# Sliding-window attention and a SwiGLU block: softmax denominators pre-added and inverted as exp(-ln), SiLU as one function, projection and scores in one phase, weights cast by DMA

## Chip, cores, metric

One core of one Trainium2 chip. The metric is the device time of the program in microseconds (us); lower is better. The span in a profile is a little shorter than that time (496.8 against 498.5 us in the profiled run of the changed kernel).

## The reference

```python
# q, k, v: (8, 8, 576, 64) float32;  x: (4608, 512);  w_gate, w_val: (512, 1536);  w_out: (1536, 512)
scores = matmul(q, k^T) / 8
scores = where((0 <= i - j) & (i - j < 64), scores, -1e9)      # causal window of 64
attn = exp(scores - max);  attn = attn / (sum(attn) + 1e-9)
x = matmul(attn, v), heads side by side, batches below one another   # 4608 tokens x 512
g = x @ w_gate
out = (g / (1 + exp(-g)) * (x @ w_val)) @ w_out
```

## The kernel before

The 4608 tokens are nine tiles of 512. A tile has four head pairs. For a head pair, GpSimd casts q, k and v to bf16, TensorE transposes q and k, VectorE puts the keys block-diagonally into `kbd`, TensorE makes the scores, ScalarE takes exp, GpSimd multiplies by a mask, and TensorE makes the product with v and, with a matrix of ones, the denominators:

```python
    def products(u):
        ...
        d_ps = ps_a.tile([P, 512], FP32, name="ad_ps", tag="a")
        for c in range(2):
            nc.tensor.matmul(d_ps[:], bones[:], E[:, :, c, :], start=(c == 0), stop=(c == 1))
        r = att.tile([P, 512], FP32, name="r", tag="r")
        nc.vector.reciprocal(r[:], d_ps[:])
        nc.vector.tensor_mul(xT[t][:, p, :], o_ps[:], r[:])

    def gate_value(t, m):            # 12 per tile; 8 matmuls of 512 columns each
        ...
        nc.scalar.activation(th[:], g_ps[:], AF.Tanh, scale=0.5)
        nc.vector.scalar_tensor_tensor(sg[:], th[:], 1.0, g_ps[:], ALU.add, ALU.mult)
        nc.vector.tensor_mul(hT[t][:, m, :], sg[:], v_ps[:])     # 0.5 is in w_out

    def project(t, s, pool, tag):    # 4 per tile; 12 matmuls of 512 columns
        ...
        nc.scalar.copy(os_[:], o_ps[:])
        nc.sync.dma_start(out[...], os_[:])
```

The main loop has 36 slots, four per tile. Each slot mixes everything, so that each engine has a little of each kind of work (the slots of the first tile, which also load and cast the weights, are cut):

```python
    for w in range(NU):              # NU = 36
        t, s = divmod(w, 4)
        ...
        gate_value(t, 3 * s)
        if w + 4 < NU: products(w + 4)
        gate_value(t, 3 * s + 1)
        if w + 5 < NU: transposes(w + 5)
        project(t - 1, s, ps_o, "o")
        if w + 8 < NU: load(w + 8)   # three to four slots ahead of its use
        if w + 6 < NU: casts(w + 6)
        if w + 5 < NU: scores(w + 5)
        gate_value(t, 3 * s + 2)
```

The softmax here doesn't subtract the row's maximum and nothing guards it: scores larger than these inputs give would overflow.

## Time and profile before

| | before |
|---|---|
| time, median of 3 runs | 472.12 us (470.81 to 472.59) |
| span of the profile | 468.9 us |
| TensorE (PE), VectorE (DVE), ScalarE (ACT), GpSimd (POOL) busy | 78, 72, 31, 38% |
| one slot, one tile, in steady state | 11.54 us, 46.2 us |

From the page, the busy time of each engine, and its time in 40 slices:

```profile
PE 367.7 (78%) x2332; PEld 189.3 (40%) x2332; DVE 338.8 (72%) x380; ACT 145.2 (31%) x253; POOL 176.9 (38%) x258
...
PE   1453866738888888888888888888888888889996
...
DVE  7188798777777777777777777777777777776540
```

Matmuls are pipelined, so a busy PE is not a PE at its peak: a matmul of 512 columns is shown with some 0.38 us, but such matmuls start 0.216 us apart (four in 0.86 us).

From the timeline of one steady slot (columns: start, duration, engine, line, operation, output<-input, count, and in brackets the idle time before it and who ended it):

```profile
256.67 3.35 DVE L217 RECIPROCAL r<-ad_ps 128x512 f32<-128x512 f32 x1
...
258.36 2.75 PE L242 MATMUL o_ps<-wo,hT 128*128 128x512 bf16 x12
...
260.06 0.69 DVE L218 TENSOR_TENSOR xT<-ao_ps,r 128x512 bf16<-128x512 f32 x1
260.67 0.68 DVE L236 SCALAR_TENSOR_TENSOR sg<-th,g_ps 128x512 f32<-128x512 f32 x1
...
262.05 0.41 DVE L152 COPY kbd_94<-tp 64x512 bf16<-64x512 bf16 x1
262.47 0.43 DVE L153 COPY kbd_94<-tp 64x512 bf16<-64x512 bf16 x1
...
262.96 0.37 PE L175 MATMUL s_ps<-qT,kbd_94 128*128 128x128 bf16 x4 [1.81 <-DVE kbd_94 L153]
```

The reader sees one reciprocal take 3.35 us, VectorE do everything after it late, and TensorE stand 1.81 us waiting for the two key copies at the end of that queue. The groups and the waits say the same over the whole run (a group: busy us, mean ns of one, then idle before it and its releaser; a wait: us in total, times, longest):

```profile
L217 DVE RECIPROCAL r<-ad_ps 128x512 f32<-128x512 f32 x36 | 120.7, 3353 | 5.0 <-PE ad_ps L215 5.0
```
```profile
PE s_ps L175 <- DVE kbd_93 L153: 31.6, 16, 4.8
PE s_ps L175 <- DVE kbd_94 L153: 29.2, 15, 2.7
```

### The profile page before, as it was taken

How to read it: one execution, taken by the hardware profiler on the slowest of the kernel's cores; microseconds unless marked ns; L12 is line 12 of the kernel's file. 1: busy time of each engine (PE TensorE's matmuls, PEld its weight loads, DVE VectorE, ACT ScalarE, POOL GpSimd, SP SyncE). 2: the span in 40 equal slices, each digit the busy share in tenths (PEclk: the TensorE clock that was granted, in tenths of full speed). 3: DMA queues.
4: the chain of work that ended last, by engine and by line, in shares of the span. 5: the costliest groups of instructions: out<-in, count | busy, mean ns of one | idle time of the engine just before them, and what ended most of it. 6: DMA issues, size and time to landing. Idle time of an engine off the chain costs nothing.

```text
span 468.9 us, 6826 instructions
## 1 busy us (share of the span) xinstructions
PE 367.7 (78%) x2332; PEld 189.3 (40%) x2332; DVE 338.8 (72%) x380; ACT 145.2 (31%) x253; POOL 176.9 (38%) x258
## 2 busy tenths in 40 slices
PE   1453866738888888888888888888888888889996
PEld 0331433414444444444444444444444444444443
DVE  7188798777777777777777777777777777776540
ACT  1220222313333333333333333333333333323232
POOL 3873445424444444444444444444444433110000
PEclk9975897879999999999999999999999999999999
DMA  7965567741332355333333443233343330001012
GB/s 173 253 182 130 154 183 209 219 104 46 87 87 67 79 138 124 87 76 82 87 86 92 119 111 90 70 90 92 90 113 92 91 89 24 22 24 45 22 46 89
DMA packets 129314, 47.65 MB, mean 102 GB/s; under 512 B 119040, under 2 KB 123136, under 8 KB 129280
## 3 DMA queue, kind: packets, MB, share of 16 engines
q1 hardware_dynamic: 129280, 47.22, 39.3%
q8 instruction: 18, 0.29, 0.3%
q14 instruction: 16, 0.13, 0.1%
HBM read 37.75 MB, written 9.44 MB: 101 GB/s over the span
## 4 chain that ended last, share of the span: by engine, by line
DVE 52%; PE 35%; ACT 4%; SPq 3%; issue 2%; POOL 2%; DMA 1%; DVEq 0%; POOLq 0%; ACTq 0%
DVE r L217 24%; PE g_ps L229 14%; PE v_ps L229 9%; DVE hT L237 9%; DVE sg L236 8%; PE o_ps L242 6%; DVE xT L218 5%; PE s_ps L175 4%; ACT th L234 3%; SPq L88 2%; POOL E L183 2%; DVE kbd_93 L153 1%; DVE kbd_94 L153 1%; DVE kbd_93 L152 1%; PE ad_ps L215 1%
## 5 line engine op out<-in xcount | busy, mean ns | idle before, releaser
L183 POOL TENSOR_TENSOR E<-E,mask 128x512 bf16<-128x512 bf16 (+1 forms) x72 | 84.5, 1185 | 215.4 <-ACT E L180 215.4
L236 DVE SCALAR_TENSOR_TENSOR sg<-th,g_ps 128x512 f32<-128x512 f32 x108 | 73.9, 684 | 86.5 <-ACT th L234 86.4
L217 DVE RECIPROCAL r<-ad_ps 128x512 f32<-128x512 f32 x36 | 120.7, 3353 | 5.0 <-PE ad_ps L215 5.0
L229 PE MATMUL g_ps<-xT,wg 128*128 128x512 bf16 x432 | 115.4, 391 | 2.9 <-DVE xT L218 2.9
L229 PE MATMUL v_ps<-xT,wv 128*128 128x512 bf16 x432 | 114.3, 388 | 0.0
L234 ACT ACTIVATE th<-g_ps 128x512 f32<-128x512 f32 x108 | 64.5, 597 | 128.4 <-PE g_ps L229 128.4
L242 PE MATMUL o_ps<-wo,hT 128*128 128x512 bf16 x432 | 98.6, 379 | 0.0
L237 DVE TENSOR_TENSOR hT<-sg,v_ps 128x512 bf16<-128x512 f32 x108 | 74.2, 687 | 11.6 <-PE v_ps L229 0.6
L229 PEld LDWEIGHTS <-wv 128*128 128x128 bf16 x432 | 43.3, 100 | 57.2 <-issue 8.6
L180 ACT ACTIVATE E<-s_ps 128x512 bf16<-128x512 f32 (+1 forms) x72 | 39.1, 592 | 68.6 <-PE s_ps L175 68.6
L242 PEld LDWEIGHTS <-hT 128*128 128x128 bf16 x432 | 41.1, 98 | 44.6
L229 PEld LDWEIGHTS <-wg 128*128 128x128 bf16 x432 | 40.9, 100 | 44.5 <-issue 3.5
L175 PE MATMUL s_ps<-qT,kbd_93 128*128 128x128 bf16 (+1 forms) x160 | 14.0, 232 | 33.0 <-DVE kbd_93 L153 31.6
L149 ACT COPY qT<-tp 128x512 bf16<-128x512 bf16 x36 | 21.1, 586 | 45.6 <-PE tp L147 45.6
L175 PE MATMUL s_ps<-qT,kbd_94 128*128 128x128 bf16 (+1 forms) x128 | 10.3, 224 | 29.2 <-DVE kbd_94 L153 29.2
L147 PE MATMUL tp<-identb,q_b 128*128 128x128 bf16 x144 | 14.8, 229 | 16.9 <-POOL q_b L108 16.9
L215 PE MATMUL ad_ps<-E,bones 128*128 128x512 bf16 x72 | 23.1, 405 | 5.4 <-DVE r L217 5.4
L175 PEld LDWEIGHTS <-kbd_93 128*128 128x128 bf16 x160 | 10.8, 107 | 39.1 <-DVE kbd_93 L153 36.3
L218 DVE TENSOR_TENSOR xT<-ao_ps,r 128x512 bf16<-128x512 f32 x36 | 24.9, 692 | 1.2
L108 POOL CAST q_b<-q_f 128x512 bf16<-128x512 f32 x36 | 22.7, 630 | 6.1 <-DMA q_f<-in_q_dram 4.5
L109 POOL CAST k_b<-k_f 128x512 bf16<-128x512 f32 x36 | 22.1, 613 | 4.3 <-PE g_ps L229 3.3
L147 PEld LDWEIGHTS <-q_b 128*128 128x128 bf16 x144 | 11.3, 102 | 26.0 <-POOL q_b L108 18.2
(77 smaller groups left out, 240.7 us busy)
## 6 DMA issues: line engine op xcount, KB each, us to landing
w_f<-in_moe_w_gate_dram SPq DMA_DIRECT2D x4, 768.0 KB, 5.4
w_f<-in_moe_w_val_dram SPq DMA_DIRECT2D x4, 768.0 KB, 7.1
q_f<-in_q_dram SPq DMA_DIRECT2D x32, 96.0 KB, 3.8
k_f<-in_k_dram SPq DMA_DIRECT2D x32, 96.0 KB, 2.4
wo_f<-in_moe_w_out_dram SPq DMA_DIRECT2D x4, 768.0 KB, 6.0
q_f<-in_q_dram SPq DMA_DIRECT2D x16, 128.0 KB, 2.8
k_f<-in_k_dram SPq DMA_DIRECT2D x16, 128.0 KB, 3.2
v_f<-in_v_dram SPq DMA_DIRECT2D x16, 128.0 KB, 3.2
```

The lines of the kernel that those rows point to most:

```text
L147: nc.tensor.transpose(tp[:, i, P * c:P * c + P], x[:, c, :], identb[:])
L175: nc.tensor.matmul(s_ps[:, 64 + P * i:64 + P * i + n], kbd[t % 2][:, p, j, :], qT[:, 64 * j:64 * j + n],)
L180: nc.scalar.activation(Ef[:, 512 * h + lo:512 * h + 512], s_ps[:, lo:512], AF.Exp, scale=0.125)
L183: nc.gpsimd.tensor_mul(Ef[:, 512 * h + lo:512 * h + 512], Ef[:, 512 * h + lo:512 * h + 512], mask[:].rearrange("r m c x -> r (m c x)")[:, ...
L215: nc.tensor.matmul(d_ps[:], bones[:], E[:, :, c, :], start=(c == 0), stop=(c == 1))
L217: nc.vector.reciprocal(r[:], d_ps[:])
L218: nc.vector.tensor_mul(xT[t][:, p, :], o_ps[:], r[:])
L229: nc.tensor.matmul(ps[:], w[:, c, P * m:P * m + P], xT[t][:, c, :], start=(c == 0), stop=(c == 3),)
L234: nc.scalar.activation(th[:], g_ps[:], AF.Tanh, scale=0.5)
L236: nc.vector.scalar_tensor_tensor(sg[:], th[:], 1.0, g_ps[:], ALU.add, ALU.mult)
L237: nc.vector.tensor_mul(hT[t][:, m, :], sg[:], v_ps[:])
L242: nc.tensor.matmul(o_ps[:], hT[t][:, c, P * s:P * s + P], wo[:, c, :], start=(c == 0), stop=(c == 11),)
```

## The change

Its intent: take the reciprocal off VectorE (ln and exp on ScalarE, from one table set), use one SiLU activation for tanh and a VectorE product, halve the denominator matmuls by adding the two halves of E on GpSimd first, let the DMA cast the weights, and order the work so that activations of one table set stand together. So a tile becomes two phases: one with products(t), scores(t+1) and the whole projection of t-1, and one with the twelve gates of t.

```diff
-        for c in range(2):
-            nc.tensor.matmul(d_ps[:], bones[:], E[:, :, c, :], start=(c == 0), stop=(c == 1))
-        nc.vector.reciprocal(r[:], d_ps[:])
+        nc.gpsimd.tensor_add(F[:], E[:, :, 0, :], E[:, :, 1, :])          # in masks()
+        nc.tensor.matmul(d_ps[:], bones[:], F[:].rearrange("r m x -> r (m x)"))
+        nc.scalar.activation(ld[:], d_ps[:], AF.Ln)
+        nc.scalar.activation(r[:], ld[:], AF.Exp, scale=-1.0)
...
-        nc.scalar.activation(th[:], g_ps[:], AF.Tanh, scale=0.5)
-        nc.vector.scalar_tensor_tensor(sg[:], th[:], 1.0, g_ps[:], ALU.add, ALU.mult)
+        nc.scalar.activation(sg[:], g_ps[:], AF.Silu)
...
-        nc.scalar.copy(os_[:], o_ps[:])
+            nc.vector.tensor_copy(os_[:], o_ps[:])
...
-            nc.sync.dma_start(w_f[:], src[...])      # and a cast on VectorE
+            nc.gpsimd.dma_start(dst[:, :, f0:f1], src[...])               # casts
... (main loop, new)
+    attention(0); set_silu(); weights_gv(0, 384)
+    for m in range(3): gate_value(0, m)
+    set_exp(); attention(1); set_silu()
+    (remaining weights); loads(2); (remaining gates of tiles 0 and 1); loads(3)
+    set_exp()
+    for u in range(4):
+        cast_qk(2, u); transposes(2, u); project(0, u); scores(2, u); cast_v(2, u); masks(2, u)
+    loads(4)
+    for u in range(4):
+        cast_qk(3, u); project(1, u); transposes(3, u); products(2, u); scores(3, u)
+    set_silu()
+    for t in range(2, NT):
+        if t > 2:
+            set_exp()
+            for u in range(4):
+                products(t, u)
+                if u % 2 == 0: project(t - 1, u // 2)
+            for u in range(4):
+                if t + 1 < NT: scores(t + 1, u)
+                if u % 2 == 1: project(t - 1, 2 + u // 2)
+            set_silu()
+        if t > 2 and t + 2 < NT: loads(t + 2)        # on SP, as the stores of project()
+        for m in range(12):
+            gate_value(t, m)
+            if m % 3 == 1:
+                u = m // 3
+                if t + 1 < NT: cast_v(t + 1, u); masks(t + 1, u)
+                if t + 2 < NT: cast_qk(t + 2, u); transposes(t + 2, u)
```

Also changed: q and k are loaded for a whole tile at once, the first loads go out from SP and ScalarE, PSUM has four attention buffers instead of three, and the pools of the other tiles are resized.

More of the change, by code (lines that the diff above doesn't have):

```diff
@@ L37 @@
     NT = NTOK // 512
-    NU = NT * 4
     ctx.enter_context(tc.manual_schedule())
     cst = ctx.enter_context(tc.tile_pool(name="cst", bufs=1))
-    stage = ctx.enter_context(tc.tile_pool(name="stage", bufs=4))
-    wst = ctx.enter_context(tc.tile_pool(name="wst", bufs=4))
-    cast = ctx.enter_context(tc.tile_pool(name="cast", bufs=2))
-    att = ctx.enter_context(tc.tile_pool(name="att", bufs=3))
-    xpool = ctx.enter_context(tc.tile_pool(name="xpool", bufs=3))
+    stage = ctx.enter_context(tc.tile_pool(name="stage", bufs=2))
+    cast = ctx.enter_context(tc.tile_pool(name="cast", bufs=1))
+    att = ctx.enter_context(tc.tile_pool(name="att", bufs=2))
+    epool = ctx.enter_context(tc.tile_pool(name="epool", bufs=6))
     fsb = ctx.enter_context(tc.tile_pool(name="fsb", bufs=3))
     hpool = ctx.enter_context(tc.tile_pool(name="hpool", bufs=2))
-    ps_a = ctx.enter_context(tc.tile_pool(name="ps_a", bufs=3, space=PSUM))
+    ps_a = ctx.enter_context(tc.tile_pool(name="ps_a", bufs=4, space=PSUM))
     ps_f = ctx.enter_context(tc.tile_pool(name="ps_f", bufs=2, space=PSUM))
-    ps_o = ctx.enter_context(tc.tile_pool(name="ps_o", bufs=1, space=PSUM))
     wg = cst.tile([P, 4, DFF], BF16, name="wg")
@@ L56 @@
     kbd = [cst.tile([P, 4, 8, P], BF16, name=f"kbd{i}") for i in range(2)]
-    vbd = [cst.tile([P, 4, 8, P], BF16, name=f"vbd{i}") for i in range(2)]
+    vbd = [cst.tile([P, 4, 8, P], BF16, name=f"vbd{i}") for i in range(3)]
     identb = cst.tile([P, P], BF16, name="identb")
     bones = cst.tile([P, P], BF16, name="bones")
-    mask = cst.tile([P, 8, 2, 64], BF16, name="mask")
+    mask = cst.tile([P, 4, 2, 64], BF16, name="mask")
     def segments(t):
@@ L72, with stages @@
     staged = {}
-    def load(u):
-        t, p = divmod(u, 4)
-        q_f = stage.tile([P, 4, 2, D], FP32, name="q_f", tag="q_f")
-        k_f = stage.tile([P, 4, 2, D], FP32, name="k_f", tag="k_f")
-        v_f = stage.tile([P, 8, D], FP32, name="v_f", tag="v_f")
-        for dst, src in ((q_f, q), (k_f, k)):
-            for off, b, s0, n in segments(t):
-                o, s, left = off, s0, n
-                while left:
-                    if o % P or left < P:
-                        m, r = 64, 64
-                    else:
-                        m, r = left // P * P, P
-                    for a in range(2):
-                        nc.sync.dma_start(
-                            dst[o % P:o % P + r, o // P:o // P + max(1, m // P), a, :],
-                            src[b, 2 * p + a, s:s + m].rearrange("(c r) d -> r c d", r=r),
-                        )
-                    o, s, left = o + m, s + m, left - m
+    def stages(t):
+        q_f = stage.tile([P, 4, H, D], FP32, name="q_f", tag="q_f")
+        k_f = stage.tile([P, 4, H, D], FP32, name="k_f", tag="k_f")
+        staged[t] = [q_f, k_f]
@@ new lines, in load_head @@
+    def load_head(eng, t, i, h):
+        dst = staged[t][i]
+        src = (q, k)[i]
+        for off, b, s0, n in segments(t):
+            o, s, left = off, s0, n
+            while left:
+                m, r = (64, 64) if o % P or left < P else (left // P * P, P)
+                eng.dma_start(
+                    dst[o % P:o % P + r, o // P:o // P + max(1, m // P), h, :],
+                    src[b, h, s:s + m].rearrange("(c r) d -> r c d", r=r),
+                )
+                o, s, left = o + m, s + m, left - m
@@ new lines, in load_chunks, with load_v @@
+    def load_chunks(eng, t, i):
+        dst = staged[t][i]
+        src = (q, k)[i]
+        for off, b, s0, n in segments(t):
+            o, s, left = off, s0, n
+            while left:
+                r = min(left, P - o % P)
+                eng.dma_start(
+                    dst[o % P:o % P + r, o // P, :, :],
+                    src[b, :, s:s + r].rearrange("h r d -> r h d"),
+                )
+                o, s, left = o + r, s + r, left - r
+    def load_v(engs, t, p):
+        v_f = stage.tile([P, 8, D], FP32, name="v_f", tag="v_f", bufs=6)
@@ L93, in load @@
         for off, b, s0, n in segments(t):
             for a in range(2):
-                nc.sync.dma_start(
+                engs[a].dma_start(
                     v_f[64 * a:64 * a + 64, off // 64:(off + n) // 64],
@@ L98, in load, with cast_qk @@
                 )
-        staged[u] = (q_f, k_f, v_f)
+        staged[t, p] = v_f
     ready = {}
-    def casts(u):
-        t, p = divmod(u, 4)
-        q_f, k_f, v_f = staged.pop(u)
-        q_b = cast.tile([P, 4, P], BF16, name="q_b", tag="q_b")
-        k_b = cast.tile([P, 4, P], BF16, name="k_b", tag="k_b")
-        nc.gpsimd.tensor_copy(q_b[:], q_f[:].rearrange("r c h d -> r c (h d)"))
-        nc.gpsimd.tensor_copy(k_b[:], k_f[:].rearrange("r c h d -> r c (h d)"))
-        vb = vbd[t % 2]
+    def cast_qk(t, u):
+        if u == 0:
+            ready[t] = [
+                cast.tile([P, 4, H, D], BF16, name=n, tag=n) for n in ("q_b", "k_b")
+            ]
+        for src, dst in zip(staged[t], ready[t]):
+            nc.gpsimd.tensor_copy(dst[:, :, 2 * u:2 * u + 2, :], src[:, :, 2 * u:2 * u + 2, :])
@@ L111, in casts, with cast_v @@
+    def cast_v(t, p):
+        v_f = staged.pop((t, p))
+        vb = vbd[t % 3]
         nc.gpsimd.tensor_copy(vb[0:64, p, :, 0:64], v_f[0:64])
         nc.gpsimd.tensor_copy(vb[64:128, p, :, 64:128], v_f[64:128])
-        ready[u] = (q_b, k_b)
-    raw = {}
-    def weights_gv(s):
-        for i, src in enumerate((moe_w_gate, moe_w_val)):
-            w_f = wst.tile([P, 4, 384], FP32, name="w_f", tag="w_f")
-            nc.sync.dma_start(
-                w_f[:], src[:, 384 * s:384 * s + 384].rearrange("(c r) f -> r c f", r=P)
-            )
-            raw[i, s] = w_f
@@ L125, in casts_gv, with weights_gv @@
-    def casts_gv(s):
-        for i, dst in enumerate((wg, wv)):
-            nc.vector.tensor_copy(dst[:, :, 384 * s:384 * s + 384], raw.pop((i, s))[:])
-    def weights_o(s):
-        w_f = wst.tile([P, 3, DM], FP32, name="wo_f", tag="w_f")
-        nc.sync.dma_start(
-            w_f[:], moe_w_out[384 * s:384 * s + 384].rearrange("(c r) f -> r c f", r=P)
-        )
-        raw[2, s] = w_f
-    def casts_o(s):
-        nc.vector.tensor_scalar_mul(wo[:, 3 * s:3 * s + 3, :], raw.pop((2, s))[:], 0.5)
+    def weights_gv(f0, f1):
+        for src, dst in ((moe_w_gate, wg), (moe_w_val, wv)):
+            nc.gpsimd.dma_start(
+                dst[:, :, f0:f1], src[:, f0:f1].rearrange("(c r) f -> r c f", r=P)
+            )
@@ L139, with weights_o, transposes @@
+    def weights_o(c0, c1):
+        nc.gpsimd.dma_start(
+            wo[:, c0:c1, :],
+            moe_w_out[P * c0:P * c1].rearrange("(c r) f -> r c f", r=P),
+        )
     queries = {}
-    def transposes(u):
-        t, p = divmod(u, 4)
-        q_b, k_b = ready.pop(u)
+    def transposes(t, u):
+        q_b, k_b = ready[t]
         tp = ps_a.tile([P, 2, 512], BF16, name="tp", tag="a")
@@ L146, in transposes, with scores @@
             for c in range(4):
-                nc.tensor.transpose(tp[:, i, P * c:P * c + P], x[:, c, :], identb[:])
-        qT = att.tile([P, 512], BF16, name="qT", tag="qT")
-        nc.scalar.copy(qT[:], tp[:, 0, :])
+                nc.tensor.transpose(
+                    tp[:, i, P * c:P * c + P],
+                    x[:, c, 2 * u:2 * u + 2, :].rearrange("r h d -> r (h d)"),
+                    identb[:],
+                )
+        if u == 0:
+            queries[t] = att.tile([P, 4, 512], BF16, name="qT", tag="qT")
+        nc.scalar.copy(queries[t][:, u, :], tp[:, 0, :])
         kb = kbd[t % 2]
         kt = tp[:, 1, :].rearrange("r (j x) -> r j x", x=64)
-        nc.vector.tensor_copy(kb[0:64, p, :, 0:64], kt[0:64])
-        nc.vector.tensor_copy(kb[64:128, p, :, 64:128], kt[64:128])
-        queries[u] = qT
+        nc.vector.tensor_copy(kb[0:64, u, :, 0:64], kt[0:64])
+        nc.vector.tensor_copy(kb[64:128, u, :, 64:128], kt[64:128])
     weights = {}
-    def scores(u):
-        t, p = divmod(u, 4)
-        qT = queries.pop(u)
-        E = att.tile([P, 8, 2, 64], BF16, name="E", tag="E")
+    def scores(t, u):
+        qT = queries[t][:, u, :]
+        E = epool.tile([P, 8, 2, 64], BF16, name="E", tag="E")
         Ef = E[:].rearrange("r m c x -> r (m c x)")
@@ L165, in scores @@
             lo = 0
-            if u < 4 and h == 0:
+            if t == 0 and h == 0:
                 lo = 64
@@ L169, in scores @@
                 j = 4 * h - 1
-                kb = kbd[t % 2][:, p, j, :] if j > 0 else kbd[(t - 1) % 2][:, p, 7, :]
+                kb = kbd[t % 2][:, u, j, :] if j > 0 else kbd[(t - 1) % 2][:, u, 7, :]
                 nc.tensor.matmul(s_ps[:, 0:64], kb, qT[:, 256 * h:256 * h + 64])
@@ L176, in scores @@
                     s_ps[:, 64 + P * i:64 + P * i + n],
-                    kbd[t % 2][:, p, j, :],
+                    kbd[t % 2][:, u, j, :],
                     qT[:, 64 * j:64 * j + n],
@@ L182, in scores, with masks, products @@
             )
-            nc.gpsimd.tensor_mul(
-                Ef[:, 512 * h + lo:512 * h + 512],
-                Ef[:, 512 * h + lo:512 * h + 512],
-                mask[:].rearrange("r m c x -> r (m c x)")[:, lo:512],
-            )
-            if t < 8 and t // 4 == h:
-                nc.gpsimd.memset(E[:, t, 0, :], 0.0)
-        weights[u] = E
+        weights[t, u] = E
+    def masks(t, u):
+        E = weights[t, u]
+        Ef = E[:].rearrange("r m c x -> r (m c x)")
+        mf = mask[:].rearrange("r m c x -> r (m c x)")
+        for h in range(2):
+            lo = 64 if t == 0 and h == 0 else 0
+            part = Ef[:, 512 * h + lo:512 * h + 512]
+            nc.gpsimd.tensor_mul(part, part, mf[:, lo:512])
+        if t < 8:
+            nc.gpsimd.memset(E[:, t, 0, :], 0.0)
+        F = epool.tile([P, 8, 64], BF16, name="F", tag="F")
+        nc.gpsimd.tensor_add(F[:], E[:, :, 0, :], E[:, :, 1, :])
+        weights[t, u] = (E, F)
     xT = {}
-    def products(u):
-        t, p = divmod(u, 4)
-        E = weights.pop(u)
+    def products(t, u):
+        E, F = weights.pop((t, u))
         Ef = E[:].rearrange("r m c x -> r (m c x)")
-        if p == 0:
-            xT[t] = xpool.tile([P, 4, 512], BF16, name="xT", tag="xT")
+        if u == 0:
+            xT[t] = att.tile([P, 4, 512], BF16, name="xT", tag="xT")
+        d_ps = ps_a.tile([P, 512], FP32, name="ad_ps", tag="a")
+        nc.tensor.matmul(d_ps[:], bones[:], F[:].rearrange("r m x -> r (m x)"))
         o_ps = ps_a.tile([P, 512], FP32, name="ao_ps", tag="a")
@@ L204, in products @@
                 continue
-            vb = vbd[t % 2][:, p, j, :] if j >= 0 else vbd[(t - 1) % 2][:, p, 7, :]
+            vb = vbd[t % 3][:, u, j, :] if j >= 0 else vbd[(t - 1) % 3][:, u, 7, :]
             lo, hi = max(0, 64 * j), min(512, 64 * j + P)
@@ L212, in products @@
             first = False
-        d_ps = ps_a.tile([P, 512], FP32, name="ad_ps", tag="a")
-        for c in range(2):
-            nc.tensor.matmul(d_ps[:], bones[:], E[:, :, c, :], start=(c == 0), stop=(c == 1))
-        r = att.tile([P, 512], FP32, name="r", tag="r")
-        nc.vector.reciprocal(r[:], d_ps[:])
-        nc.vector.tensor_mul(xT[t][:, p, :], o_ps[:], r[:])
+        ld = fsb.tile([P, 512], FP32, name="ld", tag="ld", bufs=2)
+        nc.scalar.activation(ld[:], d_ps[:], AF.Ln)
+        r = fsb.tile([P, 512], FP32, name="r", tag="r", bufs=2)
+        nc.scalar.activation(r[:], ld[:], AF.Exp, scale=-1.0)
+        nc.vector.tensor_mul(xT[t][:, u, :], o_ps[:], r[:])
     hT = {}
@@ L232, in gate_value, with project @@
                 )
-        th = fsb.tile([P, 512], FP32, name="th", tag="th")
-        nc.scalar.activation(th[:], g_ps[:], AF.Tanh, scale=0.5)
         sg = fsb.tile([P, 512], FP32, name="sg", tag="sg")
-        nc.vector.scalar_tensor_tensor(sg[:], th[:], 1.0, g_ps[:], ALU.add, ALU.mult)
+        nc.scalar.activation(sg[:], g_ps[:], AF.Silu)
         nc.vector.tensor_mul(hT[t][:, m, :], sg[:], v_ps[:])
-    def project(t, s, pool, tag):
-        o_ps = pool.tile([P, 512], FP32, name="o_ps", tag=tag)
+    def project(t, s, eng=None):
+        o_ps = ps_f.tile([P, 512], FP32, name="o_ps", tag="gv"[s % 2])
         for c in range(12):
@@ L246, in project, with set_exp, set_silu, loads @@
         os_ = fsb.tile([P, 512], FP32, name="os_", tag="os_")
-        nc.scalar.copy(os_[:], o_ps[:])
+        if eng is None:
+            nc.vector.tensor_copy(os_[:], o_ps[:])
+        else:
+            nc.scalar.copy(os_[:], o_ps[:])
         nc.sync.dma_start(out[512 * t + P * s:512 * t + P * s + P, :], os_[:])
-    for u in range(4):
-        load(u)
-    weights_gv(0)
-    load(4)
+    def set_exp():
+        nc.scalar.preload_act_table_set("natural_log_exp_and_others")
+    def set_silu():
+        nc.scalar.preload_act_table_set("silu_and_others")
+    def loads(t):
+        stages(t)
+        load_chunks(nc.sync, t, 0)
+        load_chunks(nc.sync, t, 1)
+        for p in range(4):
+            load_v((nc.sync, nc.sync), t, p)
+    stages(0)
+    for u in range(4):
+        for a in range(2):
+            load_head(nc.sync, 0, 0, 2 * u + a)
+            load_head(nc.scalar, 0, 1, 2 * u + a)
+        load_v((nc.sync, nc.scalar), 0, u)
+    set_exp()
+    loads(1)
+    make_identity(nc, identb[:])
     for i in range(2):
         nc.vector.memset(kbd[i][:], 0.0)
-    make_identity(nc, identb[:])
-    for i in range(2):
-        nc.vector.memset(vbd[i][:], 0.0)
-    casts(0)
     nc.vector.memset(bones[:], 0.0)
@@ L264 @@
     nc.vector.memset(mask[:], 1.0)
+    nc.vector.memset(vbd[0][:], 0.0)
     for a in range(2):
@@ L268 @@
             out=half[:, :, 0, :], in_=half[:, :, 0, :], compare_op=ALU.is_ge, fill=0.0,
-            base=-1, pattern=[[0, 8], [-1, 64]], channel_multiplier=1,
+            base=-1, pattern=[[0, 4], [-1, 64]], channel_multiplier=1,
         )
@@ L272 @@
             out=half[:, :, 1, :], in_=half[:, :, 1, :], compare_op=ALU.is_ge, fill=0.0,
-            base=0, pattern=[[0, 8], [1, 64]], channel_multiplier=-1,
+            base=0, pattern=[[0, 4], [1, 64]], channel_multiplier=-1,
         )
-    transposes(0)
-    casts(1)
-    weights_gv(1)
-    transposes(1)
-    scores(0)
-    load(5)
-    casts(2)
-    transposes(2)
-    scores(1)
-    products(0)
-    casts(3)
-    transposes(3)
-    scores(2)
-    products(1)
-    casts_gv(0)
-    scores(3)
@@ L293 @@
-    products(2)
-    products(3)
-    casts(4)
-    for w in range(NU):
-        t, s = divmod(w, 4)
-        if w < 4:
-            gate_value(t, 3 * s)
-            transposes(w + 4)
-            if w < 2:
-                weights_gv(w + 2)
-            else:
-                weights_o(2 * w - 4)
-                weights_o(2 * w - 3)
-            load(w + 6)
-            casts(w + 5)
-            gate_value(t, 3 * s + 1)
-            if w < 3:
-                casts_gv(w + 1)
-            scores(w + 4)
-            gate_value(t, 3 * s + 2)
-            products(w + 4)
-            if w == 3:
-                for i in range(4):
-                    casts_o(i)
-                load(10)
-                load(11)
-                transposes(8)
-                casts(9)
-                scores(8)
-            continue
-        gate_value(t, 3 * s)
-        if w + 4 < NU:
-            products(w + 4)
-        gate_value(t, 3 * s + 1)
-        if w + 5 < NU:
-            transposes(w + 5)
-        project(t - 1, s, ps_o, "o")
-        if w + 8 < NU:
-            load(w + 8)
-        if w + 6 < NU:
-            casts(w + 6)
-        if w + 5 < NU:
-            scores(w + 5)
-        gate_value(t, 3 * s + 2)
@@ new lines, in attention @@
+    def attention(t):
+        for u in range(4):
+            cast_qk(t, u)
+            transposes(t, u)
+            cast_v(t, u)
+            if u:
+                scores(t, u - 1)
+                masks(t, u - 1)
+            if u > 1:
+                products(t, u - 2)
+        scores(t, 3)
+        masks(t, 3)
+        products(t, 2)
+        products(t, 3)
+    attention(0)
+    set_silu()
+    weights_gv(0, 384)
+    nc.vector.memset(vbd[1][:], 0.0)
+    nc.vector.memset(vbd[2][:], 0.0)
@@ new lines @@
+    for m in range(3):
+        gate_value(0, m)
+    set_exp()
+    attention(1)
+    set_silu()
+    for s in range(1, 4):
+        weights_gv(384 * s, 384 * s + 384)
+    for s in range(2):
+        weights_o(6 * s, 6 * s + 6)
+    loads(2)
+    for m in range(3):
+        gate_value(1, m)
+    for s in range(1, 4):
+        for t in range(2):
+            for m in range(3 * s, 3 * s + 3):
+                gate_value(t, m)
+    loads(3)
+    set_exp()
+    for u in range(4):
+        cast_qk(2, u)
+        transposes(2, u)
+        project(0, u)
+        scores(2, u)
+        cast_v(2, u)
+        masks(2, u)
@@ new lines @@
+    loads(4)
+    for u in range(4):
+        cast_qk(3, u)
+        project(1, u)
+        transposes(3, u)
+        products(2, u)
+        scores(3, u)
+    set_silu()
+    for t in range(2, NT):
+        if t > 2:
+            set_exp()
+            for u in range(4):
+                products(t, u)
+                if u % 2 == 0:
+                    project(t - 1, u // 2)
+            for u in range(4):
+                if t + 1 < NT:
+                    scores(t + 1, u)
+                if u % 2 == 1:
+                    project(t - 1, 2 + u // 2)
+            set_silu()
+        if t > 2 and t + 2 < NT:
+            loads(t + 2)
+        for m in range(12):
+            gate_value(t, m)
+            if m % 3 == 1:
+                u = m // 3
+                if t + 1 < NT:
+                    cast_v(t + 1, u)
+                    masks(t + 1, u)
+                if t + 2 < NT:
+                    cast_qk(t + 2, u)
+                    transposes(t + 2, u)
@@ L340 @@
     for s in range(4):
-        project(NT - 1, s, ps_a, "a")
+        project(NT - 1, s)
 _INS = ['q', 'k', 'v', 'moe_w_gate', 'moe_w_val', 'moe_w_out']
```

## The prediction

> **What bounds it now.** From about 101 us on, the timeline repeats every 11.54 us (output copies at 249.62, 261.15, 272.69), 46.2 us per 512-token tile. A slot has about 9.7 us of TensorE issue: 24 gate/value and 12 output matmuls at 0.216 us pitch, 2 denominator matmuls, 26 small ones at about 0.05 us. The other 1.8 us is one wait: score matmuls wait for key copies on VectorE, queued behind the 3.35 us reciprocal (waits view: 29 to 32 us per buffer; chain of waits: reciprocal 24%). The first 101 us are DVE/DMA-bound.
>
> **What changes.**
> DVE loses 120.7 us of reciprocal, 73.9 us of (tanh+1)*g and 15.6 us of weight casts, gains 36 output copies of about 0.69 us: 339 to about 155 us busy. ACT loses 21 us of output copies, gains 72 activations of about 0.6 us and some 18 table loads. The Trainium skill, "ScalarE: Activation LUTs", What ACT_TABLE_LOAD costs, gives 1283 ns; this trace's one load took 1.28 us. PE loses 36 512-column matmuls (7.8 us). POOL gains 36 additions, estimated 1.15 us each like the masking multiply, and weight-DMA issue.
>
> **Critical path, steady state.** PE per tile: 12x1.73 + 4x2.59 + 1.8 + 1.9 + 2.7 = about 37.5 us, plus an estimated 1.4 us for PSUM rotation in the merged phase: 39 against 46.2. That alone saves some 45 us over the last six or seven tiles.
>
> **What gives it back.**
> 1. Loads. For tiles 3 to 6 the q/k loads of t+2 stand on SP behind the last output store of the merged phase, so they start when the gates of t start; the transposes of t+2 stand after the second gate, 3.5 us later. q and k are 2.1 MB in 256-byte pieces; this trace moves such pieces at about 245 GB/s at full DMA share (101 GB/s at 0.41), so 8.6 us, plus about 2 us to landing, 1.4 us of store ahead and casts: 13 us. PE stops about 10 us and restarts at a lower granted clock (skill, "TensorE: Matmul & The Clock Gate", Part 1; here matmul pitch is 0.42 us after the wait ending at 101 us, 0.216 later): about 11.5 us per tile, four tiles, 46 us.
> 2. Start. POOL does cast, mask, memset, add in series with PE and ACT: about 6.6 us per head pair in attention(0) and (1), without gates beside; POOL issues weights only after each attention. Projection of tile 0 with scores of tile 2 is a loop cast-transpose-project-score-mask, about 9 us per pair. I get: first gates at about 42 us, tiles 0 and 1 gated by 113, gates of tile 2 from 170.
> Sum: 170 + 22.5 + 4x50.5 + 37 + 34 + 14 = about 480 us span, +3 us (median over span), + a little for slow casting DMAs.
>
> **Prediction: 485 us, range 455 to 515. Chances: faster 0.17, same 0.25, slower 0.58.**
>
> **What would show it.** Right: in tiles 3 to 6, transposes wait about 10 us for POOL casts that wait for q/k DMA; granted clock dips there; tiles 7 and 8 take 34 to 39 us; DVE below 45% busy; POOL the main releaser of PE before 170 us. Wrong: no such wait (tile period 39 us throughout), or weights so late that the gates of tiles 0 and 1 starve.
>
> **What would make it wrong.** Loads not blocked behind stores: about 440 us. Casting DMAs at half rate, or long descriptor work on POOL: 500 or more.

## The result

| | before | changed |
|---|---|---|
| time, median | 471.93 us (4 runs) | 500.14 us (4 runs, 498.51 to 500.79) |
| ratio, 95% interval | | 1.061 [1.058, 1.064]: slower |
| span | 468.9 us | 496.8 us |
| PE, DVE, ACT, POOL busy | 78, 72, 31, 38% | 75, 33, 38, 44% |
| mean granted clock | 0.960 | 0.912 |

The changed kernel's page:

```profile
PE 373.0 (75%) x2255; PEld 194.1 (39%) x2296; DVE 163.9 (33%) x261; ACT 187.7 (38%) x306; POOL 218.7 (44%) x304
...
PE   1344457996457839993899479956995599999996
...
PEclk9999877999778969998799969996999599999999
DMA  9969449950208530019401950186016901101102
```

VectorE has lost half its work, as intended. But the PE row now has holes at a regular distance, with a lower clock behind each and the DMA engines, idle for a while, at full load in them. The waits (us in total, times, longest):

```profile
PE tp L145 <- POOL q_b L118: 65.0, 14, 8.7
POOL q_b L118 <- DMA q_f<-in_q_dram: 44.1, 4, 11.1
POOL k_b L118 <- DMA k_f<-in_k_dram: 17.1, 4, 4.4
...
PE s_ps L177 <- DVE kbd L156: 14.3, 6, 8.1
...
DVE os__1435 L256 <- DMA out_dram<-os__1247: 10.1, 1, 10.1
```

The casts wait for q four times and for k four times: in tiles 3 to 6. Here are the two of tile 3 in the timeline, from the last output store of the merged phase on (the phase that holds the projection):

```profile
224.83 0.33 SPq L259 DMA_DIRECT2D out_dram<-os__1918  x1
...
225.21 3.37 SPq L93 DMA_DIRECT2D q_f<-in_q_dram  x5
...
226.50 1.03 PE L239 MATMUL v_ps<-xT,wv 128*128 128x512 bf16 x3
...
228.62 4.61 SPq L93 DMA_DIRECT2D k_f<-in_k_dram  x5
232.36 0.61 POOL L118 CAST q_b<-q_f 128x512 bf16<-128x512 f32 x1 [10.96 <-DMA q_f<-in_q_dram]
...
233.02 0.61 PE L145 MATMUL tp<-identb,q_b 128*128 128x128 bf16 x4 [5.50 <-POOL q_b L118]
...
237.37 0.61 POOL L118 CAST k_b<-k_f 128x512 bf16<-128x512 f32 x1 [4.40 <-DMA k_f<-in_k_dram]
...
238.03 0.61 PE L145 MATMUL tp<-identb,k_b 128*128 128x128 bf16 x4 [4.40 <-POOL k_b L118]
...
238.44 1.91 PE L239 MATMUL g_ps<-xT,wg 128*128 128x512 bf16 x4
```

SP issues tile 5's loads only after the store of 224.83, which stands before them in the program (a1 and d3 below test this). The k pieces have landed and are cast 12 us later. TensorE stands for 5.5 and 4.4 us, and the first four gate matmuls after that take 1.70 us to issue (238.44 to 240.14) instead of 0.86. The Trainium skill, "TensorE: Matmul & The Clock Gate", Part 1, says that the clock falls to one half after an idle window of about 3.4 us and comes back after as long a busy one; this trace agrees in kind: the ten gate matmuls from 238.44 to 242.28 us start 0.43 us apart, and from about 242.6 us on the pitch is 0.216 us, some 4.5 us after TensorE began again.

The waits at the start have other owners. The longest key wait (8.1 us) and the wait of the output copy, in the last two lines of the waits above, are one event. It is seen best from SP's own queue, in the group of waits below (six; its longest, 37.5 us, is another one, which ends at 127 us):

```profile
SPq L103 <- POOL vbd L124: 48.2, 6, 37.5
```
```profile
160.53 18.29 SPq L103 DMA_DIRECT2D v_f<-in_v_dram  x16
...
173.84 0.61 POOL L118 CAST q_b<-q_f 128x512 bf16<-128x512 f32 x1 [8.30 <-PE tp L145]
...
178.92 0.55 SPq L259 DMA_DIRECT2D out_dram<-os__1247  x1
...
181.40 0.69 DVE L256 COPY os__1435<-o_ps 128x512 f32<-128x512 f32 x1 [10.11 <-DMA out_dram<-os__1247]
182.01 0.41 DVE L155 COPY kbd<-tp 64x512 bf16<-64x512 bf16 x1
182.43 0.43 DVE L156 COPY kbd<-tp 64x512 bf16<-64x512 bf16 x1
...
182.91 0.55 PE L177 MATMUL s_ps<-qT,kbd 128*128 128x128 bf16 x4 [8.06 <-DVE kbd L156]
```

Read from the top: the v loads of tile 4 stand on SP and wait for a v buffer; the cast that would free it stands on GpSimd behind a cast that waits for a transpose; so three copied output tiles wait to be stored and hold all three output buffers; the fourth output copy on VectorE has no free buffer; and the key copies stand behind that copy. TensorE waits 8.06 us for those keys, then starts slowly. This is the first fault turned round: stores behind loads instead of loads behind stores.

The stations that the prediction named, with what the timeline shows (start of the first matmul of each):

| | predicted | measured |
|---|---|---|
| first gates begin | 42 | 44.9 |
| tiles 0 and 1 gated | 113 | 116.8 |
| gates of tile 2 begin | 170 | 184.1 |
| gates of tile 2 | 22.5 | 24.1 |
| tiles 3, 4, 5, 6 | 50.5 each | 50.8, 50.9, 51.1, 51.2 |
| tile 7, tile 8 | 37, 34 | 36.4, 33.7 |
| last projection and store | 14 | 14.5 |
| span | 480 | 496.8 |

### The profile page after: what moved, and what is told of

Same layout as the page of the kernel before. It is cut to its first block, busy times and chain, and to the rows that moved or that the text cites. A ratio compares the mean times of both kernels' runs of the same rounds, so it can differ in the third digit from the quotient of the medians.

```text
span 496.8 us, 6222 instructions
## 1 busy us (share of the span) xinstructions
PE 373.0 (75%) x2255; PEld 194.1 (39%) x2296; DVE 163.9 (33%) x261; ACT 187.7 (38%) x306; POOL 218.7 (44%) x304
## 4 chain that ended last, share of the span: by engine, by line
PE 64%; POOL 10%; DMA 9%; SPq 7%; issue 6%; ACT 3%; DVE 1%; ACTq 1%; POOLq 0%; DVEq 0%
PE g_ps L239 19%; PE v_ps L239 18%; PE o_ps L250 17%; DMA k_f<-in_k_dram 6%; SPq L93 6%; POOL E L195 5%; PE tp L145 3%; PE ao_ps L219 2%; PE s_ps L177 2%; DMA wv<-in_moe_w_val_dram 2%; ACT E L182 2%; POOL q_b L118 1%; POOL k_b L118 1%; PE ad_ps L210 1%; SPq L103 1%
## 5 line engine op out<-in xcount | busy, mean ns | idle before, releaser
L195 POOL TENSOR_TENSOR E<-E,mask 128x512 bf16<-128x512 bf16 (+1 forms) x72 | 81.0, 1145 | 137.4 <-ACT E L182 135.9
L239 PE MATMUL g_ps<-xT,wg 128*128 128x512 bf16 x416 | 118.4, 404 | 7.4 <-DMA wg<-in_moe_w_gate_dram 6.2
L244 ACT ACTIVATE sg<-g_ps 128x512 f32<-128x512 f32 x108 | 64.5, 597 | 121.4 <-PE g_ps L239 120.1
L239 PEld LDWEIGHTS <-wg 128*128 128x128 bf16 x432 | 43.7, 104 | 57.4 <-issue 10.3
L155 DVE COPY kbd<-tp 64x512 bf16<-64x512 bf16 x36 | 15.0, 416 | 100.1 <-ACT qT L152 100.1
L199 POOL TENSOR_TENSOR F<-E 128x512 bf16<-128x512 bf16 x36 | 41.3, 1148 | 2.9
L177 PE MATMUL s_ps<-qT,kbd 128*128 128x128 bf16 (+1 forms) x288 | 23.8, 232 | 14.3 <-DVE kbd L156 14.3
L225 ACT ACTIVATE ld<-ad_ps 128x512 f32<-128x512 f32 x36 | 21.5, 597 | 24.1 <-PE ad_ps L210 24.0
L145 PE MATMUL tp<-identb,k_b 128*128 128x128 bf16 x144 | 17.0, 253 | 17.6 <-POOL k_b L118 17.4
L118 POOL CAST k_b<-k_f 128x512 bf16<-128x512 f32 x36 | 22.2, 615 | 17.1 <-DMA k_f<-in_k_dram 17.1
L219 PEld LDWEIGHTS <-vbd 128*128 128x128 bf16 x320 | 22.9, 108 | 17.2 <-issue 11.8
## 6 DMA issues: line engine op xcount, KB each, us to landing
wv<-in_moe_w_val_dram POOLq DMA_DIRECT2D x4, 384.0 KB, 10.5
```

The source lines that it names most:

```text
L118: nc.gpsimd.tensor_copy(dst[:, :, 2 * u:2 * u + 2, :], src[:, :, 2 * u:2 * u + 2, :])
L145: nc.tensor.transpose(tp[:, i, P * c:P * c + P], x[:, c, 2 * u:2 * u + 2, :].rearrange("r h d -> r (h d)"), identb[:],)
L177: nc.tensor.matmul(s_ps[:, 64 + P * i:64 + P * i + n], kbd[t % 2][:, u, j, :], qT[:, 64 * j:64 * j + n],)
L195: nc.gpsimd.tensor_mul(part, part, mf[:, lo:512])
L199: nc.gpsimd.tensor_add(F[:], E[:, :, 0, :], E[:, :, 1, :])
L219: nc.tensor.matmul(o_ps[:, lo:hi], vb, Ef[:, e0:e0 + hi - lo], start=first, stop=(j == 7), skip_group_check=True,)
```

## The experiments

Theories. A: the new arithmetic is sound and pays; three faults of order give it back: (1) loads behind stores on SP in tiles 3 to 6, (2) stores behind loads once at 165 to 182 us, (3) a serial ring of cast, transpose, projection, score and mask at the start. B, the rival: GpSimd's work (6.1 us per head pair) or the DMA rate bounds the changed kernel, so that moving instructions only moves the wait. C, a rival for the gain: the parts of the change themselves are worth little, because VectorE was not what bound the kernel before.

### a1: q and k loads ahead of the stores

```diff
         if t > 2:
+            if t + 2 < NT:
+                loads_qk(t + 2)
             set_exp()
...
-            loads(t + 2)
+            loads_v(t + 2)
```

> The changed kernel, with the q and k loads of tile t+2 issued at the head of tile t's merged phase, ahead of its output stores; v loads stay. Theory (loads too late): the two waits of about 5.7 and 4.3 us in each of tiles 3 to 6 vanish and with them the slow restart; tile period 50.9 to 38.5 us, total 500 to about 450 us. Rival (GpSimd work of 6.1 us per head pair, or DMA rate, sets the period of these tiles): the wait only moves to a later transpose, period stays above 45 us, total above 475 us.

Measured: 446.94 us (445.25 to 448.22), 0.948 [0.944, 0.951] of the kernel before; 53.2 us less than the changed kernel. All eight waits are gone: the only wait over 0.6 us that is left in such a tile is 0.70 us for a score buffer.

```profile
216.66 0.19 PE L173 MATMUL s_ps<-qT,kbd 128*128 128x64 bf16 x1 [0.70 <-ACT E L182]
```

Engine times in stretches of one tile (us; PE, PEld, DVE, ACT, POOL busy, granted clock, DMA share, GB/s), first tile 3 of the changed kernel, then of this one:

```profile
208.00:259.00 51.00, 40.13 (x254) 20.76 (x258) 17.27 (x29) 21.08 (x36) 23.45 (x32) 0.90 0.40 83
```
```profile
208.00:247.00 39.00, 38.03 (x259) 20.27 (x261) 17.33 (x29) 21.68 (x36) 23.38 (x32) 1.00 0.50 109
```

Nearly the same busy time of every engine, in 12 us less. GpSimd is 23.4 us busy per tile and does not bind; neither does the DMA at half load. Theory A1 stands, B falls for these tiles.

### d3: the stores from another engine

```diff
-        nc.sync.dma_start(out[...], os_[:])
+        nc.scalar.dma_start(out[...], os_[:])
```

> The changed kernel with one word changed: output stores issued from ScalarE instead of SP, so that loads and stores no longer stand in one line. Theory (the loads of tiles 5 to 8 are late only because they stand behind stores on SP, and the stores of tile 1 stand behind v loads): both waits vanish without moving any load in the program; tile period 38 to 40 us, total about 440 us (435 to 450). Rival (position of the loads in the program, or a buffer, not the shared line): tile period stays near 50 us, total 490 us or more.

Measured: 451.76 us (450.76 to 452.19), 0.958 [0.955, 0.961]. No load was moved in the program; yet the waits for q and k and the 8.06 us wait for the keys are all absent, and the tile period is 39.3 us (score waits at 216.34 and 255.66). So in tiles 3 to 6 it is the shared line that made the loads late and not their place in the program. The start gained nothing, though: the gates of tile 2 begin at 184.5 us, as in the changed kernel (184.1), which puts the total 1.8 us above the range. ScalarE now waits in order for each output copy (its exp of the scores waited 4.61 us for one at 157 us), and the ring at the start is mostly 11 to 12 us per pair instead of 10.5.

### a2: the v loads of tile 4 behind the stores

```diff
-    loads(4)
+    loads_qk(4)
     for u in range(4):
         cast_qk(3, u); project(1, u); transposes(3, u); products(2, u); scores(3, u)
+    loads_v(4)
```

> The changed kernel, with the v loads of tile 4 issued after the loop that projects tile 1 instead of before it. Theory (at 165 to 182 us the output stores stand on SP behind v loads that wait for buffers, the output copy on VectorE waits for a store, and the key copies stand behind it): the 8.1 us score wait vanishes, total down 8 to 9 us to about 491 us. Rival (GpSimd's masks and casts release those scores): no change, 499 to 501 us.

Measured: 488.70 us (488.43 to 490.01), 1.037 [1.034, 1.040]; 11.4 us less than the changed kernel (10.0 us between the two profiled spans), the expected 8 to 9 and a little more. The 8.06 us wait is gone; the same matmul waits 0.71 us:

```profile
175.72 0.37 PE L177 MATMUL s_ps<-qT,kbd 128*128 128x128 bf16 x4 [0.71 <-DVE kbd L156]
```

The gates of tile 2 begin at 176.4 instead of 184.1 us, and take 22.3 instead of 24.1 us because TensorE comes to them without the slow restart (0.43 us per matmul at the beginning of these gates in the changed kernel, 0.216 here). Theory A2 stands.

### a3: the casts of tile 2 ahead of its masks

```diff
     for u in range(4):
         cast_qk(2, u)
+        cast_v(2, u)
+    for u in range(4):
         transposes(2, u)
         project(0, u)
         scores(2, u)
-        cast_v(2, u)
         masks(2, u)
```

> The changed kernel, with the casts of q, k and v of all four head pairs of tile 2 put ahead of the loop that projects tile 0, so that no cast waits for a mask. Theory (the loop cast-transpose-project-score-mask is one serial ring of 10.5 us per pair): the loop from 117 to 157 us shrinks to about 18 us, total down about 20 us to 480 us. Rival (GpSimd's total work or the cold TensorE clock sets the loop): less than 8 us gained.

Measured: 477.68 us (477.50 to 480.79), 1.015 [1.010, 1.020]; 22.5 us less than the changed kernel. The ring is visible in the changed kernel's timeline as transposes 10.5 us apart, each behind a wait for a cast that stood behind the masks of the pair before, and between them a projection that begins at half the rate (12 matmuls in 4.1 us instead of 2.59):

```profile
135.97 0.40 PE L145 MATMUL tp<-identb,q_b 128*128 128x128 bf16 x4 [4.79 <-POOL q_b L118]
136.53 0.60 PE L145 MATMUL tp<-identb,k_b 128*128 128x128 bf16 x4 [0.16 <-POOL k_b L118]
136.92 4.27 PE L250 MATMUL o_ps<-wo,hT 128*128 128x512 bf16 x12
...
146.44 0.40 PE L145 MATMUL tp<-identb,q_b 128*128 128x128 bf16 x4 [4.79 <-POOL q_b L118]
```

With the casts ahead the pairs follow one another every 3.5 us. In the changed kernel GpSimd stood idle from 86 to 121 us; a3 does the casts of the other three pairs there, from 86.0 to 93.3 us. Theory A3 stands.

### c1: the three edits together

> The three edits together: q/k loads of t+2 at the head of the merged phase, v loads of tile 4 behind the stores, casts of tile 2 ahead. Theory (three separate faults in three separate stretches, the rest of the change sound): the gains add, 500.1 less 53.2, 11.4 and 22.4 gives about 413 us, 12% faster than the kernel before; tile period 38.5 us. Rival (the waits hide one another, or the new arithmetic is itself no gain): 430 us or more.

Measured: 416.61 us (415.30 to 419.58), 0.885 [0.881, 0.889]. The gains add up to within 4 us (500.1 - 53.2 - 11.4 - 22.5 = 413.0). The faults were separate, and without them the change is 12% faster than the kernel before.

### c2: exp(-ln) undone in c1

```diff
-        nc.scalar.activation(ld[:], d_ps[:], AF.Ln)
-        nc.scalar.activation(r[:], ld[:], AF.Exp, scale=-1.0)
+        nc.vector.reciprocal(r[:], d_ps[:])
```

> All three edits, with exp(-ln) on ScalarE undone: the reciprocal of 3.35 us back on VectorE. Theory (in the merged phase four reciprocals and four output copies are about 19 us of VectorE in a phase of 15.7 us, and hold the score and product buffers): about 6 us more in each of tiles 3 to 8, total about 445 us (range 435 to 455). Rival (VectorE at a third busy has room for 120 us, so the move to ScalarE is worth nothing once the tanh product is gone): within 5 us of the run with all three edits.

Measured: 470.50 us (469.78 to 470.70), 0.998 [0.996, 1.000]. The whole gain of c1 over the kernel before goes with it, although VectorE has less than half of the old work. Direction right, size short by 25 us. Steady tiles take 44.9 us against 38.2, about as expected; scores wait 2.65 us for a reciprocal to free its PSUM buffer:

```profile
247.47 0.19 PE L173 MATMUL s_ps<-qT,kbd 128*128 128x64 bf16 x1 [2.65 <-DVE r L225]
```

The spans differ by 53.7 us. Of these 12.5 us are lost before the products of tile 3 (189.55 against 177.01 us), which I had not counted; there the gates wait for products (2.97 us at 85 us and 2.94 us at 166 us are two such waits). The other 41 us are lost in tiles 3 to 8. My "about 6 us more in each" of these six tiles already makes 36 us, more than the 28 us that a total of 445 us allows.

### b2: the reciprocal's length taken out of the kernel before

```diff
-        nc.vector.reciprocal(r[:], d_ps[:])
+        nc.vector.tensor_copy(r[:], d_ps[:])    # wrong result on purpose
```

> The kernel before, with the reciprocal replaced by a plain copy of the same size (a wrong result on purpose): takes 2.66 us of VectorE time out of each slot and leaves every dependence. Theory (the reciprocal's length makes the hole of 1.8 us per slot): slot 11.54 to about 9.8 us, total about 410 to 420 us. Rival (the slot is bound by TensorE or by other latency): under 20 us gained.

Measured: 425.60 us (424.61 to 427.22), 0.903 [0.900, 0.906]; a wrong result, as intended. A late slot is 9.55 us (output copies at 309.83 and 319.38) without a wait of TensorE. The total is some 6 us above the range; elsewhere GpSimd's casts now wait for q, k and v loads, and TensorE waits for the masks on GpSimd (21.8 us in 15 waits). That one makes the other is likely and not tested. So the length of the reciprocal made the hole in each slot, and a copy in its place is worth 46 us by itself.

### d2: exp(-ln) in the kernel before

```diff
-        nc.vector.reciprocal(r[:], d_ps[:])
+        nc.scalar.activation(ld[:], d_ps[:], AF.Ln)
+        nc.scalar.activation(r[:], ld[:], AF.Exp, scale=-1.0)
```

> The kernel before with only the reciprocal replaced by Ln and Exp on ScalarE, tanh kept, so that each slot pays two table loads (2.6 us of ScalarE). Theory (VectorE's 3.35 us block makes the hole, and the ScalarE chain of load, ln, load, exp is 3.8 us long but blocks only ScalarE, which has room): slot 11.54 to between 10.2 and 11 us, total 435 to 455 us. Rival (the length of the chain from denominators to xT is what counts, not the engine): within 8 us of the kernel before.

Measured: 439.79 us (439.35 to 440.92), 0.933 [0.931, 0.936], with a right result. The slot is 10.61 us (score waits at 254.42 and 265.03), and the wait in it 0.88 us instead of 1.81. The table loads did not undo the gain, though there are 72 of them, each 1283 ns:

```profile
254.42 0.37 PE L175 MATMUL s_ps<-qT,kbd 128*128 128x128 bf16 x4 [0.88 <-DVE kbd L153]
...
L217 ACT ACT_TABLE_LOAD x36 | 46.2, 1283 | 0.6
L219 ACT ACT_TABLE_LOAD x36 | 46.2, 1283 | 0.6
```

This is two lines of the change in the old order of work, and it is 60 us faster than the whole change. The slot is still 1.06 us longer than b2's. Theory C falls for the reciprocal: moving it pays in both orders (53.9 us in c2, 32 us here).

### c3: the pre-addition undone in c1

```diff
-        nc.gpsimd.tensor_add(F[:], E[:, :, 0, :], E[:, :, 1, :])
-        nc.tensor.matmul(d_ps[:], bones[:], F[:].rearrange("r m x -> r (m x)"))
+        for c in range(2):
+            nc.tensor.matmul(d_ps[:], bones[:], E[:, :, c, :], start=(c == 0), stop=(c == 1))
```

> All three edits, with the pre-added denominators undone: two ones-matmuls per head pair on TensorE, no addition on GpSimd. TensorE gains 36 x 0.216 = 7.8 us; GpSimd loses 41 us, of which about 1.1 us per head pair stood on the path in the attention of tiles 0 and 1. Theory (the addition pays in steady state and costs about the same at the start): within 4 us of the run with all three edits. Rival (GpSimd is critical in steady state): 8 us or more faster than it. Other rival (the matmul is what counts): 7 us or more slower.

Measured: 408.06 us (407.82 to 409.74), 0.866 [0.863, 0.868]; 8.6 us less than c1 (6.4 us between the profiled spans), so not within 4 us. The number is the one that I had given to the rival, "GpSimd is critical in steady state", but the trace does not show that rival. Each steady tile is longer, 39.06 against 38.2 us, just the four matmuls of 0.216 us. But the first score wait of the steady part comes at 175.69 instead of 186.39 us: the addition of 1.15 us per pair stands in the ring of cast, score and mask in the attention of tiles 0 and 1 and costs 10.7 us there. So the addition on GpSimd is free in steady state and dear at the start.

### c4, d1, d4: the start mended

c4 is c1 with the casts of tiles 0 and 1 ahead of their masks, the first weight slices issued behind the casts of tile 0, and all first loads on SP (in the changed kernel ScalarE was held by its share of them until its table load at 13.36 us):

```diff
     def attention(t):
         for u in range(4):
             cast_qk(t, u)
-            transposes(t, u)
             cast_v(t, u)
+        if t == 0:
+            weights_gv(0, 384)
+        for u in range(4):
+            transposes(t, u)
...
-            load_head(nc.scalar, 0, 1, 2 * u + a)
-        load_v((nc.sync, nc.scalar), 0, u)
+            load_head(nc.sync, 0, 1, 2 * u + a)
+        load_v((nc.sync, nc.sync), 0, u)
```

> All three edits, and a mended start: in the attention of tiles 0 and 1 all casts ahead of all masks, the first weight slices issued behind the casts of tile 0 instead of behind its masks, and all first loads on SP so that ScalarE is not held issuing them until 13.4 us. Theory (the start loses some 15 us to the ring of cast and mask on GpSimd and to late weights): first gates at about 35 instead of 45 us, tile 1's attention about 6 us shorter, total about 398 us. Rival (DMA bandwidth bounds the start): under 5 us gained.

Measured: 402.02 us (401.60 to 405.18), 0.854 [0.851, 0.858]; 14.6 us less than c1; the three edits of the start were not run one by one. What now holds the start is the sum of casts, masks and additions on GpSimd (denominators waited 8.3 us for an addition at 23.9 us).

d1 is c4 with the pre-addition undone, as in c3:

> The run with the mended start, with the pre-added denominators undone as well. In the run without the pre-addition steady tiles were 39.06 instead of 38.2 us and the start 10.7 us shorter. Theory (the start stays bound by GpSimd's sum of casts and masks, so each addition taken out there counts): about 9 us less start, 5 us more steady state, total about 397 us (394 to 400). Rival (with casts ahead the additions are hidden): 405 to 408 us.

Measured: 397.54 us (397.43 to 398.48), 0.844 [0.841, 0.846]. As expected: the additions still count at the start, where the gates of tile 2 begin at 130.4 instead of 139.8 us.

d4 is c4 with the mask, its memset and the addition on VectorE instead of GpSimd (`nc.gpsimd` replaced by `nc.vector` in three calls of `masks()`):

> The run with the mended start, with mask, memset and pre-addition moved from GpSimd to VectorE. Theory (GpSimd alone holds the start; VectorE is a third busy): the waits for masked weights in the first 66 us shrink, 15 to 20 us gained, steady tiles stay 38.2 us, total about 384 us (378 to 392). Rival (the start is then held by loads, ScalarE and VectorE): under 6 us gained, or steady tiles get longer.

Measured: 384.31 us (384.14 to 384.63), 0.815 [0.813, 0.817], the fastest run here. Its groups show the mask at 485 ns and the addition at 495 ns on VectorE, against 1146 and 1151 ns on GpSimd in c4; steady tiles stay at 38.2 us. Its page:

```profile
PE   0757689999878999999999999999999999999995
```

The slices are 9.57 us long (span 382.8 us): TensorE is busy half or more of every slice from the second on, where the changed kernel had 0.3 to 0.5 until the sixth slice. With the loads as in c4, the run is 17.7 us shorter than c4, and the gates of tile 2 begin 17.1 us earlier (122.7 against 139.8 us). So these operations on GpSimd, and not the loads, held that part of the start. Whether it was their length or the queue behind them the run does not separate.

## Why the prediction was right, and where it was not

- **Slower, by late loads: right, and shown.** The prediction put the wait at about 10 us and the cost at 11.5 us per tile for tiles 3 to 6. The waits are 5.5 + 4.4 us, the tiles 50.8 to 51.2 us against 38.2 us in a1, so 12.6 to 13 us each. a1 and d3 show the cause from two sides. The direction rests on this term: a1, without these waits, is 5% faster than the kernel before.
- **Steady tile without the wait: right.** 39 us expected, 38.2 us measured in a1; tiles 7 and 8 as predicted. That the 50.5 us per tile came out so close is partly luck: the tile without the wait was put 0.8 us too long and the cost of the wait 1.1 to 1.5 us too small. VectorE at 33% is below the 45% named.
- **The reciprocal as the maker of the old hole: right.** b2 and d2 show it.
- **The step that failed: item 2, "Start", with its "gates of tile 2 from 170".** The loss was put at 13 us (485 us) and came out at 28 (500). The span's sum was 480 against 496.8, and 14.1 of the 16.8 us were in place by that step, which was reached at 184.1 us. The late loads of item 1 are not at fault: tiles 3 to 6 took 204.0 us in all against 202. Three terms of the start were too small or missing:
  - First gates at 44.9 instead of 42 us: TensorE waited 6.2 us for the first gate weights, which GpSimd issued at 37.2 us. By the end of the gates of tiles 0 and 1 the start was 3.8 us late (116.8 against 113).
  - The ring was put at "about 9 us per pair", 36 us for four pairs. The four took 40.0 us (116.8 to 156.8): after the first, 10.4 to 10.7 us each, with a projection at half the rate (4.1 us instead of 2.59 for 12 matmuls) after a wait of 4.8 us. The prediction names the slow restart for tiles 3 to 6 and not here. That makes 4.0 us more.
  - From there the prediction leaves 21 us to the gates of tile 2; it took 27.3, or 6.3 us more. No term stood for stores behind v loads: I looked for loads behind stores on SP and found them, and did not look for the reverse. It cost 7.7 us by the start of those gates and 1.8 us in them (a2), 11.4 us in the whole run; without it (a2) this stretch takes 19.3 us, less than the prediction left.
- **Casting DMAs at fault: not the cause of the rest.** After the first slices there was no wait for weights in the changed kernel. A test with the old weight path was not made, so what the casting DMA is worth stays open; so does SiLU against tanh by itself, and so does the order in two phases: what separates c1 from d2 is several parts of the change at once.

## What to carry to other kernels

When work is regrouped into phases, walk along each issuing queue as well as each engine: in these traces everything on it went in program order, so a load behind a store waits for the result that is stored, and a store behind a load waits for the buffer that is loaded. Price the start apart from steady state, since work that is free on an idle engine in steady state can be in the critical ring there (the addition in c3: 10.7 us). And try the smallest part of a change in the old order first: here two lines gave 7%, while the whole as it stood lost 6%.

## What the Trainium skill lacked or had wrong

- "ScalarE: Activation LUTs", What ACT_TABLE_LOAD costs, gives 1283 ns for the load plus about 1380 ns of drain, some 2.66 us per switch. The load is 1283 ns in all 18 of the changed kernel; no drain of that size shows: at tile 4 a SiLU ended at 258.93, the load began at 258.95 and the next Ln at 260.24, so a switch cost about 1.3 us. That Ln and Exp share a set (same page, Table sets: the hidden batching unit) is confirmed: they run back to back with no load between (0.60 and 0.63 us).
- "TensorE: Matmul & The Clock Gate", Back-to-back issue gap, gives about 131 ns per matmul of 512 columns as the sustained rate of weight load and matmul pairs. Here such pairs start 216 ns apart in the steady tiles (in a1, groups of four begin 0.86 to 0.87 us apart), which is the figure that the page gives for a single gap.
- "VectorE: DVE Perf Modes" gives no duration for the reciprocal. Here 128x512 fp32 from PSUM took 3353 ns, nearly five times the 690 ns of a product of that size.
- "DMA: Bandwidth & Descriptors" gives no rate for casting DMAs. Here 768 KB of fp32 weights arrived as 384 KB of bf16 a median 8.6 us (gate) and 10.5 us (value) after issue, and GpSimd spent 0.75 to 0.95 us on each.
- The same page, Issuing engines are not separate DMA queues, calls the issue time of a DMA usually small beside the transfer. One issue of 128 KB took 0.55 to 0.84 us here against 4.9 to 5.1 us to landing, which agrees; what the page lacks is that they add up. Twelve in a row took from 0.80 to 13.3 us on ScalarE, 8.0 us of it in issues and the rest in gaps whose cause the trace does not show, and its first table load came at 13.36 us.
